# Attention and two feed-forward layers on one core: a planner that models the VectorE and GpSimd lock and traced durations, with 233 recorded priority moves in place of 400 random draws

## The chip, the core and the metric

One core of a Trainium2 chip runs the whole program in one launch. The metric is device time in microseconds (us). TensorE (PE) multiplies matrices, VectorE (DVE), ScalarE (ACT) and GpSimd (POOL) do elementwise work, and SyncE (SP) issues all transfers between main memory and on-chip memory. Each engine works through its own instructions in the order in which they were written; semaphores hold an instruction until what it needs is there.

## The reference

The inputs are q, k and v of shape (4, 8, 576, 64), and the weights of two layers for 2304 tokens of width 512:

```python
q_rot, k_rot = (rotate(q), rotate(k))
scores = scale * np.matmul(q_rot, k_rot.transpose(0, 1, 3, 2))
scores = scores - np.max(scores, axis=-1, keepdims=True)
attn = np.exp(scores)
attn = attn / (np.sum(attn, axis=-1, keepdims=True) + 1e-09)
x = np.matmul(attn, v)        # then heads side by side: (2304, 512)
h = (x @ w1) * (x @ w2) @ w3  # width 1024
x = h @ w_out                 # width 512
h = max(x @ u1, x @ u2, x @ u3)   # width 768
return h @ u_out
```

rotate turns the two halves of each head's 64 columns by position-dependent angles. The second layer's weights are called u here. The weights are 64-bit floats.

## The kernel before, in words

**Precision.** A value is kept as two parts, HI (the value cast to fp32r) and LO (the rest), and a product takes three matmuls (TERMS, HI x HI, LO x HI and HI x LO). So nearly every matrix is split once: a ScalarE cast for HI, and a subtraction on VectorE or GpSimd for LO. The 64-bit weights are turned into 32-bit floats by `convert` (lines 365 to 392) and `to_f32` (from line 749): a load of 512 KB, a ScalarE operation on the high words (line 383), a VectorE shift of the low words (line 385) and a VectorE shift and or (line 387; lines 759 and 761 in `to_f32`), and then the split (lines 389 and 391).

**Stages.** The attention works on 16 pairs of heads (4 batches of 4). For each, `prepare` rotates q and k (lines 490 and 492) and splits them (496, 497; line 500 copies a corner with GpSimd), `score` multiplies them into two score banks, VectorE takes the row maximum (538) and ScalarE the exponential (541), which leaves its row sum by a second instruction. `move` transposes the probabilities on TensorE (546) and splits them into `pt` by ScalarE (583) and VectorE (584), and `values` multiplies `pt` with v into `pv`; `collect`, `inverse` and `rows_done` scale and split the result. What TensorE does between these steps is other work that is ready: `fold` multiplies w_out by w3 beforehand (the folds), and `gates` computes (x @ w1) * (x @ w2) of a batch as soon as its four pairs are done, and stores it. After the attention come the remaining folds (line 711 on), `y_unit` (the folded matrix times the gates), `u_group` (the second layer by Strassen's scheme with 7 products, lines 906 to 933) and the output product, which ScalarE copies out at line 992. All matmuls carry line 320 of a helper, all transfers line 323.

**What sets the order.** The kernel writes no engine's order by hand. Every step is a task of a class `Plan`: an engine, a duration in us, what it reads and writes, and a priority. `Plan.order` (line 135) plays the tasks through a model: each engine takes the ready task of lowest priority number, a task ends after its duration, a transfer ends after a latency and a time by its size (lines 190 to 193), and the shared banks of the accumulation memory are given out as they come free. `Plan.issue` (line 219) plays the model 400 times with randomly changed priorities, keeps the order whose last TensorE task ends first in the model, and writes the instructions in that order. The same order sets which task gets which bank. All this happens while the program is built. The functions at lines 257 to 275 give durations by columns. Which engine does a task is fixed (`either`, line 362). Buffers are rings: a task that would overwrite a buffer waits for all the users of its last content, SyncE's loads included.

```python
dma = max(dma, end + 0.65) + 1.4 * k.tail
end = dma + 2.8
```

Of the kernel before, what the change touches and what calls it, by code (L numbers as in the profile page):

```python
# [45 lines left out]

class Task:
    __slots__ = ("eng", "dur", "emit", "prio", "tail", "deps", "after", "out", "next", "fresh", "shared", "num")
# [29 lines left out]
class Plan:  # L78
# [9 lines left out]
    ORDERS = 400  # L88
# [45 lines left out]

    def order(self, prio):
# [16 lines left out]
        dma, done = 0.0, []  # L152
# [3 lines left out]
        while len(done) < len(tasks):  # L156
# [17 lines left out]
            if k.fresh:  # L174
# [44 lines left out]
    def issue(self):  # L219
# [16 lines left out]
        draw = random.Random(0)  # L236
        best = prio = None
        for n in range(self.ORDERS):
            if n == 0:
                p = [k.prio for k in self.tasks]  # L240
            elif n < self.ORDERS // 5:
                by = draw.choice((0.05, 0.1, 0.2, 0.3))
                p = [k.prio + draw.gauss(0, by) for k in self.tasks]
            else:
                by, share = draw.choice((0.1, 0.3, 0.6)), draw.choice((0.003, 0.01, 0.03, 0.1))
                p = [x + draw.gauss(0, by) if draw.random() < share else x for x in prio]
            o = self.order(p)
            if o and (best is None or o[0] <= best[0]):
                best, prio = o, p
# [23 lines left out]
def c_pool(n):  # L273
    return 0.3 + 0.0022 * n
# [3 lines left out]
def fused_kernel(ctx, tc, qk, vv, cs, w3t, wo, w12, m2, wo2, out):  # L278
# [43 lines left out]
    def load(o, src, us, r=(), w=(), part=(), deps=(), prio=0.0):  # L322
        return add("SP", .5, lambda: sync.dma_start(o(), src()), r, w, part, deps, prio, tail=us)  # L323
# [41 lines left out]
    def convert(src, dst, c, prio, ring=None):  # L365
# [12 lines left out]
        def cols():  # L378
# [3 lines left out]
        early = ring is None and len(cw_r.all) <= 28  # L382
        add("ACT", 0.68, lambda: act.activation(w.t, hi_word().bitcast(F32), **SHRINK),
            r=[raw], w=[w], prio=prio)
        add("DVE", 0.85 if early else 0.43, lambda: dve.tensor_scalar(low_word(), low_word(), 29, None, ALU.logical_shift_right),  # L385
            part=[raw], deps=raw.writers, prio=prio)
        add("DVE", 1.15 if early else 0.69, lambda: dve.scalar_tensor_tensor(  # L387
            u(), u(), 3, low_word(), ALU.logical_shift_left, ALU.bitwise_or), r=[raw], w=[w], prio=prio)
# [3 lines left out]
            r=[w, dst], part=[dst], prio=prio)  # L392

    def split(dst, sel, n, prio, eng="DVE"):
# [5 lines left out]
            r=[dst], part=[dst], deps=dst.writers[-1:], prio=prio)  # L400
# [58 lines left out]
    for z in zs:  # L459
        add("POOL", 0.3, lambda z=z: pool.memset(f32(z.t), 0.0), w=[z], prio=-1)  # L460
# [4 lines left out]
    def prepare(p):  # L465
# [5 lines left out]
        for e in (1, 0):  # L471
# [12 lines left out]
            if p == 0 and e == 0:  # L484

                for i in range(2):
# [4 lines left out]
                        r=[tb[i]], part=[t], deps=[get[i]], prio=prio) for i in range(2)]  # L491
            k = add(eng, cost(S), lambda t=t, on=on: on.tensor_tensor(t.t[:, 0], t.t[:, 0], t.t[:, 1], ALU.add),
                    part=[t], deps=last, prio=prio)
# [4 lines left out]
                st.t[:, lo], t.t[:, 0], f32(st.t[:, hi]), ALU.subtract), part=[t, st], deps=[k], prio=prio)  # L498
# [4 lines left out]
    def prepare_v(p):  # L503
# [6 lines left out]
            r=[r, v], part=[v], prio=prio)  # L510
# [4 lines left out]
    def score(p, part, j):  # L515
# [16 lines left out]
        add("PE", 6 * c_mm(288) + (0.0 if common else 0.2), go, r=[st, z] if common else [st], w=ss, prio=prio)  # L532
        for e, s in enumerate(ss):
# [7 lines left out]
            add("ACT", 0.84, lambda s=s, col=col, o=o: act.activation(  # L541
# [208 lines left out]
    def to_f32(srcs, prio):  # L750
# [3 lines left out]
        for src, n in srcs:  # L754
# [4 lines left out]
        add("DVE", 0.5, lambda: dve.tensor_scalar(raw.t[:, :, 0], raw.t[:, :, 0], 29, None, ALU.logical_shift_right),  # L759
            part=[raw], deps=raw.writers, prio=prio)  # L760
        add("DVE", 0.87, lambda: dve.scalar_tensor_tensor(
            w.t.bitcast(U32), w.t.bitcast(U32), 3, raw.t[:, :, 0], ALU.logical_shift_left, ALU.bitwise_or),
            r=[raw], w=[w], prio=prio)
# [29 lines left out]
    def u_weights(n, w, t):  # L793
        prio = P2 + (7 if n < 2 else 20) + n
        d = us[n] = next_slot([128, 2, 7, 128], "u")
        for sel, lo, hi, src in ((lambda: w.t[:, :384], 0, 3, w), (lambda: t.t, 3, 7, t)):
# [4 lines left out]
                r=[src], part=[d], deps=[k], prio=prio)  # L801
# [5 lines left out]
    def y_unit(at, u):  # L807
# [27 lines left out]
        for kk in range(2):  # L835
# [22 lines left out]
            for t, c, deps in ((x, S1, [ks1, ks3]), (z, S2, [ks2, ks4])):  # L858
# [4 lines left out]
                    part=[yc], deps=[k], prio=prio)  # L863
# [20 lines left out]
    def u_group(n, grp, at):  # L884
# [43 lines left out]
        def out(o, e, t):  # L928
# [4 lines left out]
            add("DVE", c_dve(TN), lambda: dve.tensor_tensor(t.t, t.t, e.t, ALU.max), r=[e], w=[t], prio=prio)  # L933
# [130 lines left out]
```

## Time and profile before

| | |
|---|---|
| median of 3 runs (lowest to highest) | 942.92 us (942.62 to 944.05) |
| the profiled execution | 944.48 us |
| its span, first to last instruction | 942.5 us |
| instructions | 16352 |
| TensorE matmul busy | 898.9 us (95%), 6018 |
| TensorE weight loads busy | 835.4 us (89%) |
| VectorE busy | 613.3 us (65%), 1048 |
| ScalarE busy | 493.5 us (52%), 1108 |
| GpSimd busy | 398.6 us (42%), 387 |
| mean granted TensorE clock | 0.992 |

The profiled execution is one of its own; its span is what the engines show, and 1.98 us lie around it. Busy time counts an instruction from its start to its end. Matmuls are pipelined, so the next one starts while the one before still counts as busy, and a busy TensorE is not one at its peak. The time of a VectorE or GpSimd instruction includes what it waits for inside the engine. Of a wait the profile tells which instruction, as far as semaphores show, ended it. Granted clock 1.00 is 2.4 GHz, 0.50 is 1.2 GHz.

### The profile page before, as it was taken

Reading aid. Unit: us, or ns where it says so; the run is one execution under the profiler, and the core shown is the slowest. Engines: PE = TensorE matmul, PEld = TensorE weight load, DVE = VectorE, ACT = ScalarE, POOL = GpSimd, SP = SyncE. Lnnn points to the kernel's source line nnn. Section 1 sums busy time; section 2 is a strip of 40 time slices with the busy share of each in tenths; the row PEclk is TensorE's granted clock in tenths of the full one; section 3 lists DMA queues with packets and bytes.
Section 4 is the critical chain, followed back from the end, with each engine's and each line's share of the span. In section 5 each row is a group of like instructions: output and inputs, shape, how many; then the busy total and the mean of one; then the engine's idle time right before and its main releaser. Section 6 shows DMA issues by size and latency. Waiting matters only on the chain.

```text
span 942.5 us, 16352 instructions
## 1 busy us (share of the span) xinstructions
PE 898.9 (95%) x6018; PEld 835.4 (89%) x6018; DVE 613.3 (65%) x1048; ACT 493.5 (52%) x1108; POOL 398.6 (42%) x387
## 2 busy tenths in 40 slices
PE   2789999999999999999999999999989999999998
PEld 1667778889999999899998999999989999999886
DVE  6888989887666665666657332656687577588300
ACT  4688887776666665766644232434432322334411
POOL 1788889756665455632110000424563333342000
PEclk9799999999999999999999999999999999999999
DMA  7444556453232122210128543333233214155511
GB/s 250 129 152 144 163 156 199 152 155 113 99 96 85 59 85 89 97 40 27 34 101 254 181 133 101 92 102 96 67 112 112 79 46 137 54 174 185 201 68 67
DMA packets 61088, 110.32 MB, mean 117 GB/s; under 512 B 6736, under 2 KB 39760, under 8 KB 61008
## 3 DMA queue, kind: packets, MB, share of 16 engines
q1 hardware_dynamic: 61008, 109.28, 36.5%
q8 instruction: 47, 0.77, 0.3%
q14 instruction: 33, 0.27, 0.1%
HBM read 83.76 MB, written 25.50 MB: 116 GB/s over the span
## 4 chain that ended last, share of the span: by engine, by line
PE 79%; DVE 11%; ACT 5%; issue 3%; DMA 1%; POOL 1%; SPq 0%; DVEq 0%; ACTq 0%
PE q L320 45%; PE m L320 15%; PE t L546 7%; PE s L320 6%; PE pv L320 6%; DVE pt L584 3%; DVE sm L538 2%; ACT pt L583 2%; DVE cw L387 1%; DVE raw L385 1%; DMA tabs__119<-in_cs_dram 1%; POOL ga L784 1%; SPq L323 0%; DVE sm L551 0%; DMA r_d<-rt 0%
## 5 line engine op out<-in xcount | busy, mean ns | idle before, releaser
L584 DVE TENSOR_TENSOR pt<-t,pt 128x320 fp32r<-128x320 f32 (+3 forms) x256 | 132.6, 527 | 66.5 <-ACT pt L583 62.7
L583 ACT CAST pt<-t 128x320 fp32r<-128x320 f32 (+3 forms) x256 | 112.8, 457 | 54.1 <-PE t L546 35.2
L538 DVE TENSOR_REDUCE sm<-s 128x1 f32<-128x576 f32 x144 | 104.0, 750 | 17.1 <-PE s L320 16.0
L320 PE MATMUL pv<-pt,v 128*128 128x256 f32 (+1 forms) x576 | 110.3, 313 | 4.5 <-DVE pt L584 4.5
L320 PE MATMUL q<-gt,wp 128*128 128x384 f32 x576 | 100.0, 334 | 0.0
L320 PEld LDWEIGHTS q<-gt,wp 128*128 128x128 f32 x576 | 99.8, 188 | 0.0
L320 PE MATMUL s<-st 64*128 64x288 f32 x768 | 73.2, 319 | 19.0 <-ACT st L496 13.2
L320 PEld LDWEIGHTS pv<-pt,v 128*128 128x128 f32 x576 | 83.1, 191 | 8.9 <-DVE pt L584 6.1
L320 PEld LDWEIGHTS s<-st 64*128 64x128 f32 x768 | 56.4, 193 | 32.3 <-ACT st L496 13.2
L906 ACT COPY tmp<-q 128x384 f32<-128x384 f32 x54 | 25.9, 479 | 100.7 <-PE q L320 100.1
L320 PE MATMUL q<-yc__7826,u 128*128 128x384 f32 x378 | 70.8, 339 | 1.0 <-DVE tmp L932 1.0
L320 PE MATMUL q<-yc__8092,u 128*128 128x384 f32 x378 | 70.6, 339 | 1.1 <-DVE top L909 1.1
L320 PE MATMUL q<-yc__7547,u 128*128 128x384 f32 x378 | 71.1, 339 | 0.5 <-DVE tmp L909 0.4
L320 PEld LDWEIGHTS q<-yc__8092,u 128*128 128x128 f32 x378 | 66.6, 188 | 1.8 <-DVE top L909 1.5
L320 PEld LDWEIGHTS q<-yc__7826,u 128*128 128x128 f32 x378 | 66.7, 188 | 1.3 <-DVE tmp L932 1.3
L320 PEld LDWEIGHTS q<-yc__7547,u 128*128 128x128 f32 x378 | 66.2, 188 | 1.8 <-DVE tmp L909 0.7
L919 POOL TENSOR_TENSOR tmp<-tmp 128x384 f32<-128x384 f32 x27 | 29.8, 1103 | 89.9 <-ACT tmp L906 89.9
L320 PE MATMUL q<-tail,tail 128*128 128x512 f32 x216 | 49.1, 389 | 0.0
L320 PEld LDWEIGHTS q<-tail,tail 128*128 128x128 f32 x216 | 40.6, 188 | 8.4
L398 DVE TENSOR_TENSOR gt<-gt 128x768 fp32r<-128x768 f32 x24 | 25.5, 1068 | 27.0 <-ACT gt L397 27.0
L847 POOL TENSOR_TENSOR yx<-yc__7547 128x384 f32<-128x384 f32 x2 | 2.7, 1338 | 89.5 <-DVE yc__7547 L831 87.3
L992 ACT COPY ga<-q 128x512 f32<-128x512 f32 x18 | 10.6, 588 | 56.6 <-PE q L320 48.5
(1282 smaller groups left out, 2173.7 us busy)
## 6 DMA issues: line engine op xcount, KB each, us to landing
gt<-g_d SPq DMA_DIRECT2D x24, 384.0 KB
raw<-in_m_dram SPq DMA_DIRECT2D x72, 128.0 KB
raw<-in_w_dram SPq DMA_DIRECT2D x16, 512.0 KB
h_d<-top SPq DMA_DIRECT2D x36, 192.0 KB
tail<-h_d SPq DMA_DIRECT2D x36, 192.0 KB
raw<-in_wo_dram SPq DMA_DIRECT2D x12, 512.0 KB
raw<-in_w3t_dram SPq DMA_DIRECT2D x12, 512.0 KB
vr<-in_vv_dram SPq DMA_DIRECT2D x16, 320.0 KB
```

The lines of the kernel that those rows point to most:

```text
L320: pe.matmul(o, a, b, start=start, stop=stop, **kw)
L385: add("DVE", 0.85 if early else 0.43, lambda: dve.tensor_scalar(low_word(), low_word(), 29, None, ALU.logical_shift_right), part=[raw], de ...
L387: add("DVE", 1.15 if early else 0.69, lambda: dve.scalar_tensor_tensor(u(), u(), 3, low_word(), ALU.logical_shift_left, ALU.bitwise_or), r ...
L398: add(eng, c_dve(n) if eng == "DVE" else c_pool(n), lambda: e.tensor_tensor(sel()[:, LO], f32(sel()[:, LO]), f32(sel()[:, HI]), ALU.subtract),
L538: add("DVE", c_dve(S), lambda s=s, col=col: dve.tensor_reduce(sm.t[:, 0, col:col + 1], s.t[:, :, :288], axis=AX.XY, op=ALU.max, negate=Tru ...
L546: pe.transpose(o, x, ident.t)
L583: h = add("ACT", c_evac(n), lambda: act.copy(hi(), t.t[:rows, a:a + n]), r=[t], w=[pt], prio=prio)
L584: add("DVE", c_dve(n), lambda: dve.tensor_tensor(low(), t.t[:rows, a:a + n], f32(hi()), ALU.subtract), r=[t], part=[pt], deps=[h], prio=prio)
L784: return add("POOL", c_pool(128), lambda: pool.tensor_tensor(q(i), x(), y(), ALU.subtract), r=[w], part=[t], deps=deps, prio=prio)
L906: add("ACT", c_evac(TN), lambda: act.copy(d.t, ps(o)), r=[accs[o]], w=[d], prio=prio)
L919: add("POOL", c_pool(TN), lambda: pool.tensor_tensor(s5.t, s1.t, s5.t, ALU.add), r=[s1], w=[s5], prio=prio)
L992: add("ACT", c_evac(512), lambda acc=acc, o=o: act.copy(o.t, acc.t), r=[acc], w=[o], prio=P2 - 2)
```

## The change

Three things change, all in the planner. (1) A task may be marked `lock`: all GpSimd tasks but the two first fills are, and of VectorE's tasks those that work from on-chip main memory to it (the splits from it, the conversions, the rotation, the maxima of line 933, the small addition of line 551). In the model a marked task starts only when the marked task before it has ended, on whichever engine. (2) Durations: GpSimd by columns, the conversions, the exponential, a pair of scores, the small addition, an issue by SyncE, and the model of a transfer. (3) In place of 400 random draws the priorities are changed by 233 recorded moves, each given by a seed: a seed picks a stretch of the order, a share of its tasks and how far their priorities go. Then one order is played and written. The same tasks stay on the same engines. The diff, cut (some 20 more lines only add `lock=True`):

```diff
--- before.py
+++ after.py
@@ -1,5 +1,4 @@
-import random
@@ -44,8 +43,67 @@
+MOVES = (
+    100000004, 100000005, 100000020, 100000029, 100000035, 100000038, 100000041, 100000063, 100000085, 100000086,
...
+    100172746, 100174918, 100175949,
+)
+
+
+def draws(seed):
+    mask = (1 << 64) - 1
+    s = (seed * 0xD1342543DE82EF95 + 1) & mask
+    while True:
+        s = (s + 0x9E3779B97F4A7C15) & mask
+        z = ((s ^ (s >> 30)) * 0xBF58476D1CE4E5B9) & mask
+        z = ((z ^ (z >> 27)) * 0x94D049BB133111EB) & mask
+        yield z ^ (z >> 31)
+
+
+def move(prio, place, seed):
+
+    d = draws(seed)
+
+    def uni():
+        return (next(d) >> 11) * (1.0 / 9007199254740992.0)
+
+    by = (0.1, 0.3, 0.6, 1.5)[next(d) >> 62]
+    share = (0.01, 0.03, 0.1, 0.3)[next(d) >> 62]
+    parts = (1, 8, 32, 128)[next(d) >> 62]
+    width = len(prio) / parts
+    lo = uni() * (len(prio) + width) - width
+    hi = lo + width
+    if parts == 1:
+        share *= 0.3
+    for i in range(len(prio)):
+        if lo <= place[i] < hi and uni() < share:
+            x = uni() + uni() + uni() + uni() - 2.0
+            prio[i] = prio[i] + by * 1.7 * x
+
+
...
-    ORDERS = 400
...
-    def add(self, eng, dur, emit, r=(), w=(), part=(), deps=(), prio=0.0, tail=0.0):
+    def add(self, eng, dur, emit, r=(), w=(), part=(), deps=(), prio=0.0, tail=0.0, lock=None):
...
+        k.lock = eng == "POOL" if lock is None else lock
...
-        dma, done = 0.0, []
+        dma, port, done = 0.0, 0.0, []
...
+            if k.lock:
+                at = max(at, port)
             end = at + k.dur
+            if k.lock:
+                port = end
             clock[e] = end - LAP[e]
             if e == "PE":
                 end += self.DRAIN
             if k.tail:
-                dma = max(dma, end + 0.65) + 1.4 * k.tail
-                end = dma + 2.8
+                dma = max(dma, end + 0.65) + 1.2 * k.tail
+                end = dma + 0.8
...
-        draw = random.Random(0)
-        best = prio = None
-        for n in range(self.ORDERS):
...
+        prio = [k.prio for k in self.tasks]
+        place = {k.num: i for i, k in enumerate(self.order(prio)[1])}
+        for seed in MOVES:
+            move(prio, place, seed)
+        best = self.order(prio)
...
 def c_pool(n):
-    return 0.3 + 0.0022 * n
+    return 0.18 + 0.00216 * n
...
-        return add("SP", .5, lambda: sync.dma_start(o(), src()), r, w, part, deps, prio, tail=us)
+        return add("SP", .42, lambda: sync.dma_start(o(), src()), r, w, part, deps, prio, tail=us)
...
-        early = ring is None and len(cw_r.all) <= 28
...
-        add("DVE", 0.85 if early else 0.43, lambda: dve.tensor_scalar(low_word(), low_word(), 29, None, ALU.logical_shift_right),
-            part=[raw], deps=raw.writers, prio=prio)
-        add("DVE", 1.15 if early else 0.69, lambda: dve.scalar_tensor_tensor(
-            u(), u(), 3, low_word(), ALU.logical_shift_left, ALU.bitwise_or), r=[raw], w=[w], prio=prio)
+        add("DVE", 0.42, lambda: dve.tensor_scalar(low_word(), low_word(), 29, None, ALU.logical_shift_right),
+            part=[raw], deps=raw.writers, prio=prio, lock=True)
+        add("DVE", 0.69, lambda: dve.scalar_tensor_tensor(
+            u(), u(), 3, low_word(), ALU.logical_shift_left, ALU.bitwise_or), r=[raw], w=[w], prio=prio, lock=True)
...
-        add("PE", 6 * c_mm(288) + (0.0 if common else 0.2), go, r=[st, z] if common else [st], w=ss, prio=prio)
+        add("PE", 6 * c_mm(288) + (0.0 if common else 0.285), go, r=[st, z] if common else [st], w=ss, prio=prio)
...
-            add("ACT", 0.84, lambda s=s, col=col, o=o: act.activation(
+            add("ACT", 0.93, lambda s=s, col=col, o=o: act.activation(
...
-        a = add("DVE", 0.4, lambda: dve.tensor_scalar_add(sm.t[:, 2], sm.t[:, 1], EPS), r=[sm], part=[sm], prio=prio)
+        a = add("DVE", 0.17, lambda: dve.tensor_scalar_add(sm.t[:, 2], sm.t[:, 1], EPS), r=[sm], part=[sm], prio=prio,
+                lock=True)
...
-        add("DVE", 0.5, lambda: dve.tensor_scalar(raw.t[:, :, 0], raw.t[:, :, 0], 29, None, ALU.logical_shift_right),
-            part=[raw], deps=raw.writers, prio=prio)
-        add("DVE", 0.87, lambda: dve.scalar_tensor_tensor(
...
+        add("DVE", 0.42, lambda: dve.tensor_scalar(raw.t[:, :, 0], raw.t[:, :, 0], 29, None, ALU.logical_shift_right),
+            part=[raw], deps=raw.writers, prio=prio, lock=True)
+        add("DVE", 0.69, lambda: dve.scalar_tensor_tensor(
```

## Rows read from the trace of the kernel before

**Rows 1.** Busy time by stage: stretch and length, engines, granted clock, transfer share, GB/s.

```profile
0.00:75.00 75.00, 47.65 (x303) 38.98 (x304) 59.15 (x93) 49.98 (x113) 46.27 (x45) 0.91 0.52 170
75.00:200.00 125.00, 119.10 (x892) 102.86 (x890) 109.19 (x182) 101.22 (x244) 105.11 (x87) 1.00 0.55 169
200.00:490.00 290.00, 285.93 (x2325) 266.85 (x2325) 189.49 (x365) 190.21 (x482) 136.19 (x128) 1.00 0.23 75
490.00:660.00 170.00, 169.99 (x1036) 165.68 (x1035) 87.69 (x128) 61.59 (x105) 27.61 (x26) 1.00 0.47 142
660.00:705.00 45.00, 42.40 (x235) 40.56 (x235) 35.84 (x59) 18.69 (x37) 28.38 (x36) 1.00 0.31 94
705.00:943.00 238.00, 233.81 (x1235) 220.46 (x1233) 131.98 (x226) 71.81 (x131) 55.07 (x68) 1.00 0.33 111
```

The engines stand in the order PE, PEld (weight loads), DVE, ACT, POOL.

**Rows 2.** Waits of PE, 0 to 75 us: for whom, us in total, times, longest.

```profile
PE s L320 <- ACT st L496: 13.2, 1, 13.2
PE pv L320 <- DVE pt L584: 3.2, 5, 1.9
PE s L320 <- ACT p__209 L541: 2.5, 1, 2.5
PE s L320 <- ACT p__176 L541: 1.7, 1, 1.7
```

**Rows 3.** Waits of PE, 75 to 200 us.

```profile
PE t L546 <- DVE pt L584: 3.4, 7, 1.3
```

**Rows 4.** Waits of PE, 490 us to the end.

```profile
PE q L320 <- DVE top L909: 1.1, 1, 1.1
PE q L320 <- DVE tmp L932: 1.0, 1, 1.0
```

**Rows 5.** Instructions in order of time: start, duration, engine, idle before it.

```profile
27.84 0.28 POOL L500 CAST z__105<-st 64x128 fp32r<-64x128 f32 x1
27.87 2.20 DVE L387 SCALAR_TENSOR_TENSOR cw<-cw,raw 128x512 uint32<-128x512 uint32 x1
28.09 1.42 POOL L490 TENSOR_TENSOR qk__169<-qk__169,tabs__131 128x576 f32<-128x576 f32 x1
...
30.10 1.14 DVE L584 TENSOR_TENSOR pt<-t,pt 64x256 fp32r<-64x256 f32 x2
...
32.61 0.74 ACT L541 ACTIVATE p__314<-s,sm 128x576 f32<-128x576 f32 x1 [0.70 <-DVE sm L538]
...
33.24 0.19 ACT L541 ACTIVATION_READ_ACCUMULATOR p__314<-s,sm 128x1 f32 x1
...
34.10 1.22 PE L320 MATMUL pv<-pt,v 128*128 128x256 f32 x4 [1.95 <-DVE pt L584]
```

**Rows 6.** Conversions by line: busy us, mean ns; 0 to 75, 75 to 200, last 490 on.

```profile
L387 DVE SCALAR_TENSOR_TENSOR cw<-cw,raw 128x512 uint32<-128x512 uint32 x8 | 9.6, 1195 | 0.2
L385 DVE TENSOR_SCALAR raw<-raw 128x512 uint32<-128x512 uint32 x8 | 6.7, 843 | 0.1
...
L387 DVE SCALAR_TENSOR_TENSOR cw<-cw,raw 128x512 uint32<-128x512 uint32 x20 | 21.2, 1059 | 3.7 <-ACT cw L383 3.2
L385 DVE TENSOR_SCALAR raw<-raw 128x512 uint32<-128x512 uint32 x19 | 18.6, 984 | 0.1
...
L387 DVE SCALAR_TENSOR_TENSOR cw<-cw,rawc 128x512 uint32<-128x512 uint32 x6 | 4.1, 691 | 2.1 <-ACT cw L383 1.9
...
L385 DVE TENSOR_SCALAR rawc<-rawc 128x512 uint32<-128x512 uint32 x6 | 2.5, 421 | 0.0
```

**Rows 7.** Busy time by stretch, columns as in rows 1: the clock after a stall.

```profile
32.00:34.00 2.00, 0.16 (x2) 0.00 (x0) 1.96 (x5) 1.39 (x4) 2.00 (x3) 0.85 0.38 150
34.00:36.00 2.00, 1.90 (x10) 1.67 (x12) 1.86 (x4) 1.10 (x4) 0.86 (x1) 0.50 0.03 8
```

**Rows 8.** Instructions in order of time: a load's issue and its first use.

```profile
543.96 0.37 SPq L323 DMA_DIRECT2D gt<-g_d  x1
...
547.14 0.83 ACT L397 CAST gt<-gt 128x768 fp32r<-128x768 f32 x1 [2.29 <-DMA gt<-g_d]
```

More of the change, by code (lines that the diff above doesn't have):

```diff
@@ L43 @@
 TERMS = ((HI, HI), (LO, HI), (HI, LO))
+MOVES = (
[24 rows of a table added]
+)
[23 more added lines that the diff above has]
+            prio[i] = prio[i] + by * 1.7 * x
 class Task:
-    __slots__ = ("eng", "dur", "emit", "prio", "tail", "deps", "after", "out", "next", "fresh", "shared", "num")
+    __slots__ = ("eng", "dur", "emit", "prio", "tail", "deps", "after", "out", "next", "fresh", "shared", "num", "lock")
 class Buf:
@@ L235, in issue @@
                 d.next.append(k)
-        draw = random.Random(0)
-        best = prio = None
-        for n in range(self.ORDERS):
[L239 to L249, printed above, removed]
+        prio = [k.prio for k in self.tasks]
[3 more added lines that the diff above has]
+        best = self.order(prio)
         for b, n in best[2].items():
@@ L391, in convert @@
         add(eng, cost(512), lambda: on.tensor_tensor(cols()[:, LO], w.t, f32(cols()[:, HI]), ALU.subtract),
-            r=[w, dst], part=[dst], prio=prio)
+            r=[w, dst], part=[dst], prio=prio, lock=True)
     def split(dst, sel, n, prio, eng="DVE"):
@@ L399, in split @@
             sel()[:, LO], f32(sel()[:, LO]), f32(sel()[:, HI]), ALU.subtract),
-            r=[dst], part=[dst], deps=dst.writers[-1:], prio=prio)
+            r=[dst], part=[dst], deps=dst.writers[-1:], prio=prio, lock=True)
     wob = [slots[4 + i].new() for i in range(2)]
@@ L459, in fused_kernel @@
     for z in zs:
-        add("POOL", 0.3, lambda z=z: pool.memset(f32(z.t), 0.0), w=[z], prio=-1)
+        add("POOL", 0.3, lambda z=z: pool.memset(f32(z.t), 0.0), w=[z], prio=-1, lock=False)
     QH, QL, KH, KL = range(4)
@@ L490, in prepare @@
             last = [add(eng, cost(S), lambda i=i, t=t, on=on, tb=tb: on.tensor_tensor(t.t[:, i], t.t[:, i], tb[i].t, ALU.mult),
-                        r=[tb[i]], part=[t], deps=[get[i]], prio=prio) for i in range(2)]
+                        r=[tb[i]], part=[t], deps=[get[i]], prio=prio, lock=True) for i in range(2)]
             k = add(eng, cost(S), lambda t=t, on=on: on.tensor_tensor(t.t[:, 0], t.t[:, 0], t.t[:, 1], ALU.add),
-                    part=[t], deps=last, prio=prio)
+                    part=[t], deps=last, prio=prio, lock=True)
             eng, cost, on = either(p < 1)
@@ L497, in prepare @@
             add(eng, cost(S), lambda t=t, on=on, hi=hi, lo=lo: on.tensor_tensor(
-                st.t[:, lo], t.t[:, 0], f32(st.t[:, hi]), ALU.subtract), part=[t, st], deps=[k], prio=prio)
+                st.t[:, lo], t.t[:, 0], f32(st.t[:, hi]), ALU.subtract), part=[t, st], deps=[k], prio=prio, lock=True)
         for e, rows in enumerate(HEADS):
@@ L509, in prepare_v @@
         add(eng, cost(640), lambda: on.tensor_tensor(v.t[:, :, LO], r.t, f32(v.t[:, :, HI]), ALU.subtract),
-            r=[r, v], part=[v], prio=prio)
+            r=[r, v], part=[v], prio=prio, lock=True)
     probs = {}
@@ L758, in to_f32 @@
             r=[raw], w=[w], prio=prio)
[L759 to L761 removed]
+        add("DVE", 0.42, lambda: dve.tensor_scalar(raw.t[:, :, 0], raw.t[:, :, 0], 29, None, ALU.logical_shift_right),
+            part=[raw], deps=raw.writers, prio=prio, lock=True)
+        add("DVE", 0.69, lambda: dve.scalar_tensor_tensor(
             w.t.bitcast(U32), w.t.bitcast(U32), 3, raw.t[:, :, 0], ALU.logical_shift_left, ALU.bitwise_or),
[L763 removed]
+            r=[raw], w=[w], prio=prio, lock=True)
         return w
@@ L800, in u_weights @@
                 d.t[:, LO, lo:hi], sel().rearrange("p (a b) -> p a b", b=128), f32(d.t[:, HI, lo:hi]), ALU.subtract),
-                r=[src], part=[d], deps=[k], prio=prio)
+                r=[src], part=[d], deps=[k], prio=prio, lock=True)
     yc_r = [ring("py", [128, 7, 2, 2, TN], F32R, f"yc{g}_") for g in range(NG)]
@@ L862, in y_unit @@
                     yc.t[:, c:c + 2, kk, LO], t.t[:, 1:3], f32(yc.t[:, c:c + 2, kk, HI]), ALU.subtract),
-                    part=[yc], deps=[k], prio=prio)
+                    part=[yc], deps=[k], prio=prio, lock=True)
                 t.users += [k, k2]
@@ L932, in out @@
             add("DVE", c_dve(TN), lambda: dve.tensor_tensor(e.t, ps(o), e.t, ALU.add), r=[accs[o]], w=[e], prio=prio)
-            add("DVE", c_dve(TN), lambda: dve.tensor_tensor(t.t, t.t, e.t, ALU.max), r=[e], w=[t], prio=prio)
+            add("DVE", c_dve(TN), lambda: dve.tensor_tensor(t.t, t.t, e.t, ALU.max), r=[e], w=[t], prio=prio, lock=True)
         prod("c", S4, B22, 4)
```

22 rows, old and new, of the table MOVES are left out of this document.

## The prediction

> **What bounds the kernel now.** I read the stages first. From 490 us on TensorE is full: idle for 0.01 us of 170 up to 660, 2.6 us of 45 up to 705, and 3.7 us after that, which is the last copy and store [rows 1]. No order of the same 16,352 instructions shortens that half by more than some 2.6 us. What an order can win lies in the first 490 us, the attention: TensorE is idle for 27.35 us up to 75, 5.9 up to 200 and 4.1 up to 490. Of the first 27.35, 13.2 are the head, until the first operands are loaded, rotated and split [rows 2]; that chain uses the same loads and the same operations after the change.
>
> A busy TensorE is pipelined, so short waits hide in its busy time. I therefore compare paces. In 200 to 490 a matmul leaves every 290/2325 = 0.1247 us, its own waits included [rows 1]. At that pace the 303 matmuls up to 75 need 37.8 us; between 13.2 and 75 they took 61.8, so about **24.0 us** are lost there. The 892 up to 200 need 111.2 and took 125: **13.8 us**. (The kinds differ a little between the stretches; it is an estimate.)
>
> Then what ended those waits: the exponential that frees a score bank, and the low half of the transposed probabilities, `pt`, from VectorE line 584 [rows 2, 3]. Why line 584 is late shows in order of time [rows 5]: at 27.87 VectorE begins a weight conversion, line 387. GpSimd runs line 500 and then line 490, and the conversion ends only at 30.07. Two `pt` behind it start at 30.10 and TensorE still waits for VectorE at 34.1, 1.95 us visibly. Alone, that conversion takes 0.691 and its partner on line 385 0.421; beside GpSimd they average 1.195 and 0.843 up to 75, and 1.059 and 0.984 from 75 to 200 [rows 6]. The surplus is VectorE time spent waiting for GpSimd: 8 x 0.504 + 8 x 0.422 = 7.4 us up to 75, and 20 x 0.368 + 19 x 0.563 = 18.1 us up to 200. VectorE is busy 59 of 75 and 109 of 125 us there, so this is time on the engine that TensorE waits for. A stall costs twice: after TensorE stood nearly idle at 32 to 34 the granted clock is 0.50 at 34 to 36, the 1.2 GHz level [rows 7].
>
> **The change, part by part.** It adds and removes no instruction: every engine does the same work, each in another order. The planner runs while the kernel is built, so neither 400 drawn orders nor the replay of 233 moves costs chip time. All terms are waits that go or come.
>
> *The lock in the model.* A task that is marked starts only when the last marked one has ended, on either engine. Before, two conversions were given fixed inflated times (0.85 and 1.15 for the early ones), so the planner thought VectorE slow but could not see which GpSimd operation to avoid. Now it sees 0.42 and 0.69 plus a wait that depends on the order. The order can set the conversion before a `pt` that is not yet needed, or two locked VectorE operations side by side. The bounds of the gain in each stretch are nothing (GpSimd is busy 46 and 105 us there and the lock must be shared somehow) and the whole loss.
> - Up to 75: between 0 and 24.0. The nearest row is the surplus of the 8 conversions, 7.4 us. I take **7.0**.
> - 75 to 200: between 0 and 13.8. The surplus, 18.1, is above the loss, so the rows do not choose; GpSimd is busy 84% of the time and will keep colliding. I take half, **7.0**.
> - 200 to 490: idle is 4.1. Few conversions are left, but the same `pt` waits end it. I take **3.0**; bounds 0 and 4.1.
> - 660 to 705: 2.6 idle, with waits for line 909's and 932's results [rows 4]. I take **1.5**; bounds 0 and 2.6.
> - 490 to 660 and after 705: nothing; TensorE's queue covers all of it, and if a late load broke that cover the wait would show there one for one.
>
> *Durations.* The exponential goes from 0.84 to 0.93; its two records are 0.74 and 0.19 [rows 5]. GpSimd on 576 columns goes from 0.3 + 0.0022 x 576 = 1.57 to 1.42; the record is 1.42. These correct the order and carry no term of their own; their worth is inside the four terms, since the waits that remain come from the old figures too.
>
> *Transfers.* For a 384 KB load the model counted 0.5 + 0.65 + 1.4 x 1.1 + 2.8 = 5.49 us from issue to use; now 0.42 + 0.65 + 1.2 x 1.1 + 0.8 = 3.19. The trace has issue at 543.96 and use at 547.14: 3.18 us [rows 8]. So loads that come through a clear queue are modelled right now and may be used 2.3 us earlier. SyncE issues in order: behind a load that waits for its buffer stand all later ones, the stores of the gates too. Up to 200 the transfer engines are busy about 54% of the time [rows 1], so some loads will land later than the model says. Bounds: 0 if all were early anyway, and 2.3 us for each load that becomes the last thing ScalarE waits for. I take 0: TensorE's waits name no transfer anywhere beyond the head [rows 2 to 4].
>
> **Sum.** 7.0 + 7.0 + 3.0 + 1.5 = 18.5 us. The profiled execution took 944.48 (span 942.5, with 1.98 around it); it would take 926.0, span 924.0. The median of the runs is 942.92, 1.56 below the profiled one, so I forecast 942.92 - 18.5 = **924.4**.
>
> **Rivals.**
> *More is won.* Waits hidden by the pipeline go too, and the low clock after 34 with them: 16 of 24.0 (the first scores and `pt` of pair 0, some 8 us, have nothing to hide behind), 12 of 13.8, 4 of 4.1, 2.5 of 2.6, together 34.5: 908.4. For it: weight loads are idle for 290 - 266.85 = 23.2 us in 200 to 490, where TensorE seems idle for only 4.1 [rows 1]. Against: a long matmul keeps the next weight load waiting with nothing wrong. The Trainium skill (Trainium Kernel Development and Optimization, Performance Expectations) says that matmul busy time is a bad measure because matmuls are pipelined, and weight-load busy time a good one; by that rule alone more lies open in 200 to 490 than my 4.1, and this case would be the likelier.
>
> *Less is won.* The opening is bound by throughput: VectorE 59 of 75, GpSimd 105 and VectorE 109 of 125 [rows 1], and the folds and gates that could fill TensorE need those conversions. Then 2 + 3 + 1 + 1 = 7: 935.9. Against: ScalarE and GpSimd do stand idle in both stretches.
>
> *No change.* Waits go to other places one for one, because TensorE waits for the last of four engines. 942.9. It would also be so if the replayed moves gave an order no better than the old.
>
> *Slower: the lock passes VectorE by.* The model gives the lock in the order of asking, so a marked VectorE task waits for at most the GpSimd task then running. The row shows otherwise: asked at 27.87, GpSimd's line 500 ended at 28.12, but line 490 got in at 28.09 and VectorE ended at 30.07, against 28.12 + 0.69 = 28.81: 1.26 us later [rows 5]. An order that packs GpSimd without gaps and sets conversions just ahead of `pt` makes this happen more often, in the first 200 us. Each case holds VectorE 1.26 us with `pt` queued behind and TensorE behind that; 18.5/1.26 = 15 additional cases cancel the gain, 25 give 31.5 - 18.5 = 13 us more: 955.9. Against: line 387's mean of 1.195 up to 75 says that most cases wait for one task at most. The Trainium skill (SBUF — State Buffer, Who interferes with whom) states that whoever issues first gets the shared ports for the whole instruction; by that rule VectorE would have had them at 28.12 and this rival could not occur, but the row at 27.87 does not fit it.
>
> **How the numbers follow.** The forecast 0.55 (913 to 932: half as much again or half of the terms), more 0.15, less 0.17, no change 0.04, slower 0.09. Faster by over 0.2%, about what a measurement of this kernel can tell from no change: 0.87; within: 0.04; slower: 0.09. The range, 908 to 938, holds the first three cases with a little above the third, and leaves out the last two, 0.13.
>
> **What would show it.** In the profile after: the same busy ScalarE; VectorE's busy time shorter, with lines 385 and 387 nearer 0.42 and 0.69 up to 200; TensorE's idle up to 200 down from 33 us to 20 or so; few stretches at 0.50 after 30 us; 490 to 660 still full, ending earlier by the same amount. If lines 385 and 387 take as long as before and the time still falls, the lock was not the reason and the search or the durations were. If ScalarE's first waits are for loads up to 200, the transfer figures are too short. If conversions over 1.7 us are frequent, the lock rival is right. I am wrong in size if the stretch before 75 does not shrink.

## The result, and the profile after

The changed kernel took 933.17 us (932.24 to 935.18, 4 runs), the kernel before 943.48 on the same chip: a ratio of 0.9893, 95% interval 0.9872 to 0.9914. That is **10.3 us faster**; the forecast was 18.5 faster, at 924.4. Direction and range (908 to 938) held, the size was little over half: the time lies 1.2 us outside the band that had the most weight (913 to 932) and nearer to the rival "less is won" (935.9) than to the forecast.

Busy time by stage of the kernel after, columns and stretches as in [rows 1]; its span is 931.7 us:

```profile
0.00:75.00 75.00, 44.97 (x275) 35.65 (x275) 58.19 (x85) 46.89 (x105) 46.56 (x45) 0.91 0.50 169
75.00:200.00 125.00, 121.52 (x930) 107.70 (x930) 107.09 (x192) 105.32 (x255) 102.17 (x84) 1.00 0.54 174
200.00:490.00 290.00, 288.56 (x2373) 273.03 (x2372) 192.69 (x373) 194.87 (x490) 141.49 (x131) 1.00 0.26 82
490.00:660.00 170.00, 169.56 (x1021) 165.50 (x1020) 86.40 (x127) 62.60 (x105) 34.43 (x32) 1.00 0.41 126
660.00:705.00 45.00, 45.00 (x257) 45.00 (x256) 35.62 (x65) 17.97 (x35) 21.68 (x32) 1.00 0.33 99
```
(The stage from 705 us on is left out: TensorE is idle there for the last 3.6 us, as before.)

Read it by TensorE's idle time and by its matmuls beside [rows 1]. Idle, in the order of the stages: 30.0 (27.35 before), 3.5 (5.9), 1.4 (4.1), 0.4 (0.01), 0 (2.6). Matmuls done: at 75 us 275, 28 **fewer** than before; at 200 us 1205, 10 more; at 490 us 3578, 58 more; at 705 us 4856, 65 more. So the opening lost time, and the rest won back more than three times as many matmuls.

The kinds of matmul that are done early differ, so counts are only a guide to times. An estimate that weighs them: count each matmul with the planner's own duration for its columns (`c_mm`: 0.013 us and 0.000417 us for each column, at least 0.109). By that measure the changed kernel's TensorE is 3.6 us of work **behind** the kernel before at 75 us, and ahead by 1.5 at 200, 7.8 at 490, 7.4 at 660, 11.1 at 705 and 10.7 at its last matmul. Stage by stage that is -3.6, 5.1, 6.3, -0.4, 3.7 and -0.4 us. In the second profile of the same order (the run `again` below) it is -2.0 at 75 us and 9.5 at the end, so a single profile is good to a microsecond or two.

TensorE's waits, after, 0 to 75 us and below the dots 75 to 200 us; beside [rows 2, 3]:

```profile
PE s L373 <- ACT st L548: 13.1, 1, 13.1
PE s L373 <- ACT p__349 L593: 4.2, 2, 3.0
PE s L373 <- ACT p__208 L593: 3.4, 1, 3.4
PE t L598 <- DVE sm L605: 2.9, 2, 2.2
...
PE pv L373 <- DVE pt L637: 1.7, 2, 1.4
PE t L598 <- DVE pt L637: 0.6, 1, 0.6
```

From 75 to 200 us, the `t` waits for `pt` fall from 3.4 us in seven waits to 0.6 in one; the `pv` waits for `pt` do not fall (1.3 us before, 1.7 after). Up to 75 the waits for two score banks (`p__349`, `p__208`) alone cost 7.6 us, as much as all the waits for score banks before (7.3, the longest 2.5).

The conversions, after, 0 to 75 us and then 75 to 200 us, beside [rows 6]; lines 437 and 439 are the old 385 and 387:

```profile
L439 DVE SCALAR_TENSOR_TENSOR cw<-cw,raw 128x512 uint32<-128x512 uint32 x7 | 7.7, 1097 | 0.1
L437 DVE TENSOR_SCALAR raw<-raw 128x512 uint32<-128x512 uint32 x8 | 6.5, 829 | 0.1
...
L439 DVE SCALAR_TENSOR_TENSOR cw<-cw,raw 128x512 uint32<-128x512 uint32 x20 | 19.2, 962 | 0.9 <-ACT cw L435 0.7
L437 DVE TENSOR_SCALAR raw<-raw 128x512 uint32<-128x512 uint32 x20 | 13.8, 692 | 1.6 <-DMA raw<-in_w_dram 1.3
```

Against 0.691 and 0.421 alone, the surplus up to 75 us is 7 x 0.406 + 8 x 0.408 = 6.1 us (7.4 before), and from 75 to 200 us 20 x 0.271 + 20 x 0.271 = 10.8 (18.1 before; 12.4 in the second profile). The collisions cost less but are far from gone.

The longest of the new waits, in order of time:

```profile
16.87 0.81 DVE L542 TENSOR_TENSOR early<-early,tabs__107 128x576 f32<-128x576 f32 x1
17.48 1.47 POOL L542 TENSOR_TENSOR qk__146<-qk__146,tabs__107 128x576 f32<-128x576 f32 x1 [0.41 <-DMA qk__146<-in_qk_dram]
17.61 1.97 DVE L542 TENSOR_TENSOR early<-early,tabs__115 128x576 f32<-128x576 f32 x1
18.92 1.91 POOL L542 TENSOR_TENSOR qk__146<-qk__146,tabs__115 128x576 f32<-128x576 f32 x1
19.49 1.95 DVE L542 TENSOR_TENSOR early<-early,tabs__134 128x576 f32<-128x576 f32 x1
21.36 1.41 DVE L590 TENSOR_REDUCE sm<-s 128x1 f32<-128x576 f32 x2
22.14 0.74 ACT L593 ACTIVATE p__208<-s,sm 128x576 f32<-128x576 f32 x1 [3.70 <-DVE sm L590]
...
24.70 0.41 PE L598 MATMUL t<-ident,p__182 128*128 128x128 f32 x1
...
26.12 0.27 PE L598 MATMUL t<-ident,p__208 128*128 128x128 f32 x1
```

VectorE does three products in a row. A load lands just before 17.48, GpSimd starts on it while the first product runs, takes the lock, and from then on the two engines take turns: the second and third product take 1.97 and 1.95 us instead of 0.75. (The plan has this GpSimd product at 18.83, behind VectorE's three.) The row maxima behind them come 2.4 us late, then the exponential that frees the bank, then TensorE.

### The profile page after: what moved, and what is told of

Its sections match the earlier page's. It is cut to its first block, busy times and chain, and to the rows that moved or that the text cites. A ratio compares the mean times of both kernels' runs of the same rounds, so it can differ in the third digit from the quotient of the medians.

```text
span 931.7 us, 16391 instructions
## 1 busy us (share of the span) xinstructions
PE 892.7 (96%) x6018; PEld 836.9 (90%) x6018; DVE 601.5 (65%) x1048; ACT 495.5 (53%) x1108; POOL 397.6 (43%) x387
## 4 chain that ended last, share of the span: by engine, by line
PE 86%; DVE 6%; ACT 2%; DMA 2%; issue 2%; POOL 1%; SPq 0%; DVEq 0%; ACTq 0%
PE q L373 46%; PE m L373 17%; PE t L598 9%; PE s L373 7%; PE pv L373 7%; DVE sm L590 1%; DVE pt L637 1%; ACT pt L636 1%; DVE cw L439 1%; DMA qk__118<-in_qk_dram 1%; DMA raw<-in_w_dram 1%; DVE raw L437 1%; DMA wq_d<-fl 1%; DVE early L542 0%; DMA wp<-wq_d 0%
## 5 line engine op out<-in xcount | busy, mean ns | idle before, releaser
L373 PE MATMUL pv<-pt,v 128*128 128x256 f32 (+1 forms) x576 | 115.4, 317 | 4.5 <-DVE pt L637 3.6
L590 DVE TENSOR_REDUCE sm<-s 128x1 f32<-128x576 f32 x144 | 104.2, 749 | 17.3 <-PE s L373 16.4
L985 DVE TENSOR_TENSOR tmp<-q,tmp 128x384 f32<-128x384 f32 x54 | 29.8, 554 | 16.3 <-PE q L373 16.2
L1045 ACT COPY ga<-q 128x512 f32<-128x512 f32 x18 | 10.6, 588 | 54.8 <-PE q L373 46.7
```

Of the source, the lines that this page charges most:

```text
L373: pe.matmul(o, a, b, start=start, stop=stop, **kw)
L590: add("DVE", c_dve(S), lambda s=s, col=col: dve.tensor_reduce(sm.t[:, 0, col:col + 1], s.t[:, :, :288], axis=AX.XY, op=ALU.max, negate=Tru ...
L985: add("DVE", c_dve(TN), lambda: dve.tensor_tensor(e.t, ps(o), e.t, ALU.add), r=[accs[o]], w=[e], prio=prio)
L1045: add("ACT", c_evac(512), lambda acc=acc, o=o: act.copy(o.t, acc.t), r=[acc], w=[o], prio=P2 - 2)
```

## Experiments

### Is it the opening? A lock lost to an early load, and a low clock

Three kernels add work to the changed one and leave its order alone. The first holds GpSimd back, so that VectorE's three products run together; the second fills TensorE's wait at 35 to 38 us with transposes whose results nothing reads, to keep the clock from falling; the third does both.

```diff
+    def hold():
+        t = ap.tile([128, 512], F32, tag="hold", name="hold")
+        for _ in range(4):
+            pool.memset(t, 0.0)
...
+    def warm():
+        t = ps_m.tile([128, 512], F32, tag="bank1", name="warm")
+        for i in range(24):
+            tr(t[:, 128 * (i % 4):128 * (i % 4) + 128], ident.t)
...
         for k in best[1]:
+            if k.eng == "POOL":
+                count += 1
+                if count == 6:
+                    self.hold()
+            if k.eng == "PE":
+                turns += 1
+                if turns == 18:
+                    self.warm()
             k.emit()
```

> The changed kernel itself, so that the three kernels beside it have a baseline on the same chip. Every theory expects 0.989 of the kernel before, about 933 us, with the same profile: conversions short from 75 us on, and up to 75 us TensorE no faster than before.

> Added work only: four fills of an unused tile on GpSimd, some 2.1 us, ahead of its first rotation product at 17.48 us. Theory: a load that landed 1.35 us before the model's time let GpSimd start early and take the lock inside VectorE's planned run of three products, which took 0.81, 1.97 and 1.95 us. With GpSimd held back they take 0.75 each, TensorE's wait at 23.1 us falls from 3.4 us to about 1, and the end comes 2 to 2.6 us earlier than in the changed kernel (ratio to it 0.997 to 0.998). Rival: GpSimd is what the opening waits for; then 2.1 us more on it cost 1 to 2 us, or the gain is given back within 50 us and the ratio is 1.000.

> Added work only: 24 transposes of the identity matrix into an unused bank, in TensorE's wait between 35.4 and 38.4 us. Theory: the stall at 36 to 38 us costs a second time, because the granted clock is 0.50 from 38 to 50 us and some 9 us of matmuls take double there. With TensorE kept busy the clock stays at 1.00 and the end comes 3 to 4 us earlier (ratio to the changed kernel 0.996 to 0.997). Rival: VectorE and ScalarE set the pace up to 75 us; then the clock rises, but TensorE waits instead, and the gain is under 1 us.

> The two additions together: GpSimd held back ahead of its first rotation product and TensorE kept busy at 35 to 38 us. If both theories hold and do not share their gain, 5 to 6.5 us less than the changed kernel (ratio 0.993 to 0.995); if the opening is bound by VectorE and ScalarE, under 1.5 us.

Ratios to the kernel before, with intervals: the changed kernel again 0.9901 (0.9886 to 0.9915), 933.51 us; held 0.9893 (0.9878 to 0.9908), 933.47; warm 0.9888 (0.9871 to 0.9904), 932.97; both 0.9881 (0.9863 to 0.9898), 931.31. The intervals overlap, so none of the additions has a measured gain. With both, the median is 2.2 us below the changed kernel's, between what the theory (5 to 6.5) and the rival (under 1.5) expected, and not clear of noise. But both additions did what they were to do. The held kernel in order of time:

```profile
16.94 2.27 POOL L389 MEMSET hold<- 128x512 f32 x4
17.53 0.74 DVE L554 TENSOR_TENSOR early<-early,tabs__115 128x576 f32<-128x576 f32 x1
18.20 0.74 DVE L554 TENSOR_TENSOR early<-early,tabs__134 128x576 f32<-128x576 f32 x1
19.46 1.42 DVE L602 TENSOR_REDUCE sm<-s 128x1 f32<-128x576 f32 x2 [0.52 <-PE s L378]
21.23 1.78 PE L378 MATMUL s<-st,z__105 128*128 128x288 f32 x6 [1.57 <-ACT p__213 L605]
```

The products take 0.74, and TensorE starts the batch at 21.23 instead of 23.15. What became of it shows where TensorE starts the same matmul (counted from the first, added transposes left out) in the profile of each, in us:

| matmul | again | hold | warm | both |
|---|---|---|---|---|
| 25 | 23.15 | 21.23 | 21.36 | 21.49 |
| 139 | 49.98 | 48.75 | 47.68 | 46.32 |
| 240 | 65.76 | 65.26 | 63.55 | 63.78 |
| 294 | 75.83 | 74.97 | 75.16 | 74.98 |
| 1205 | 200.19 | 198.25 | 200.50 | 198.26 |
| 5947 | 912.82 | 911.34 | 912.18 | 912.23 |

At 50 us the two additions have won 3.7 us; at 76 us 0.7 to 0.9 is left, whichever was made. These are single profiles: the first profile of the changed kernel starts its 294th matmul at 76.67, 0.84 later than the one in the table, so differences of a microsecond or two, further down above all, rank nothing. Busy time by stretch of the kernel with both:

```profile
36.00:38.00 2.00, 1.00 (x7) 0.55 (x5) 2.00 (x4) 2.00 (x5) 0.62 (x1) 1.00 0.30 40
40.00:45.00 5.00, 3.11 (x26) 2.50 (x27) 4.03 (x7) 3.43 (x9) 5.00 (x5) 1.00 0.75 236
...
68.00:70.00 2.00, 0.97 (x5) 1.00 (x6) 2.00 (x4) 0.83 (x2) 1.55 (x3) 0.70 0.84 223
70.00:72.00 2.00, 2.00 (x7) 1.51 (x6) 1.27 (x2) 1.81 (x5) 2.00 (x2) 0.50 0.58 231
```

and two of its instructions in order of time:

```profile
69.03 0.37 PE L615 MATMUL t<-ident,sm 128*9 128x128 f32 x1 [2.16 <-DVE sm L629]
...
69.69 2.79 PE L383 MATMUL m<-ws__177,ws__588 128*128 128x512 f32 x6
```

The same stretches in the changed kernel run again (but the first):

```profile
40.00:45.00 5.00, 3.85 (x19) 3.01 (x19) 3.16 (x6) 3.23 (x9) 5.00 (x4) 0.50 0.79 265
...
68.00:70.00 2.00, 0.96 (x4) 0.48 (x3) 1.94 (x3) 0.63 (x2) 2.00 (x2) 1.00 0.81 235
70.00:72.00 2.00, 0.65 (x5) 0.66 (x6) 1.97 (x5) 0.83 (x2) 1.62 (x4) 1.00 0.88 256
```

and the same wait and six matmuls in it:

```profile
71.35 0.27 PE L598 MATMUL t<-ident,sm 128*9 128x128 f32 x1 [2.38 <-DVE sm L605]
...
71.70 1.64 PE L373 MATMUL m<-ws__177,ws__558 128*128 128x512 f32 x6
```

The clock stays at 1.00 through 36 to 45 us, where it had been 0.50. TensorE then comes earlier to its wait for VectorE's `sm`, which is its 258th matmul, and that wait too ends earlier, at 69.03 instead of 71.35. So of the 3.7 us 2.3 are left there: VectorE is ahead as well. Behind the wait the granted clock falls to 0.50, and six matmuls take 2.79 instead of 1.64; that takes 1.5 of the 2.3. A low clock was removed at one place and another came. Why it came there is open: the changed kernel stands idle at the same wait for as long (2.38 us, against 2.16) with the clock shown as 1.00 throughout, and so does the held kernel (2.14), while behind the same wait of the kernel with the transposes only (2.40) it is shown as 0.62 and 0.53.

The rival held in its result: most of the time that was won by 50 us is given back within 30 us. Of its reason, that up to 75 us TensorE follows VectorE, ScalarE and GpSimd, the profiles show a part, the 1.3 us that go between 50 us and the wait; the other 1.5 went with the clock.

One more thing shows in the run with the transposes only: VectorE got its second product through without any help (0.75 us; the third still took 1.96), and matmul 25 starts at 21.36. Everything before had come half a microsecond earlier. So not all that this run wins up to 50 us is due to its transposes, which start only at 34.42.

### Model or search?

Four kernels with the planner's search made equal: 20,000 tries of the same kind of move, each kept where it makes the planned end earlier. They differ in the model alone.

```diff
 # eq_both_new: MOVES are the 53 kept of 20,000
 # eq_no_lock: the lock is off while the moves are tried and in the order that is written
-            if k.lock:
+            if k.lock and self.LOCK:
                 at = max(at, port)
 # eq_old_durations: the lock stays
-    return 0.18 + 0.00216 * n
+    return 0.3 + 0.0022 * n
-        return add("SP", .42,
+        return add("SP", .5,
-                dma = max(dma, end + 0.65) + 1.2 * k.tail
-                end = dma + 0.8
+                dma = max(dma, end + 0.65) + 1.4 * k.tail
+                end = dma + 2.8
...
 # eq_old_model: both, and the inflated conversions of before
```

> The changed planner with a search of its own: 20,000 tried moves of the same kind, 53 of them kept, in place of the recorded 233. The control for the three beside it, which have the same number of tries. Every theory expects nearly what the changed kernel gives, 0.990 to 0.993 of the kernel before (934 to 937 us).

> The traced durations without the lock in the model, 20,000 tries, 48 kept. If the lock is what counts: VectorE's conversions take 0.9 to 1.2 us again up to 200 us and the time is 0.997 or more of the kernel before (940 us or more). If the traced durations or the search count, 0.990 to 0.993 like the control.

> The lock in the model, but the durations and the transfer figures of before (without the inflated conversions, which stood for the lock), 20,000 tries, 61 kept. If the traced durations count: 0.997 or more of the kernel before. If the lock or the search counts: 0.990 to 0.993.

> The planner's model of before, without the lock and with the old durations, but 20,000 tries in place of 400, 53 kept. If the number of tries is what counts: 0.990 to 0.993 of the kernel before. If the model counts: 0.998 to 1.002, because 50 times the search then only follows a wrong model.

Two more with the changed model and less search: no moves at all, and the 400 draws of before.

> The changed model with no move replayed: one order from the priorities as written. If the model alone made the gain, 0.990 to 0.995 of the kernel before; if the moves are needed to use it, 1.005 to 1.02, because the kernel before had the best of 400 orders and this has the first.

> The changed model, but the 400 random draws of the kernel before in place of the 233 moves. If the model is what counts and a short search is enough: 0.990 to 0.994 of the kernel before. If the recorded moves are worth as much as the model: 0.995 to 1.000.

| kernel | model | search | us | ratio (95%) | TensorE's end: planned, profiled |
|---|---|---|---|---|---|
| before | old | 400 draws | 943.48 | 1 | 914.3, 938.8 |
| after | new | 233 moves | 933.17 | 0.9893 (0.9872 to 0.9914) | 912.6, 928.1 |
| eq_old_model | old | 20,000 | 941.79 | 0.9979 (0.9969 to 0.9988) | 907.4, 936.4 |
| no_moves | new | none | 957.19 | 1.0142 (1.0125 to 1.0159) | 935.0, 952.5 |
| draws_400 | new | 400 draws | 950.45 | 1.0080 (1.0058 to 1.0103) | 928.4, 948.4 |
| eq_both_new | new | 20,000 | 933.69 | 0.9894 (0.9878 to 0.9911) | 915.8, 928.0 |
| eq_old_durations | lock, old durations | 20,000 | 947.79 | 1.0041 (1.0028 to 1.0055) | 933.4, 943.1 |
| eq_no_lock | new durations, no lock | 20,000 | 957.52 | 1.0136 (1.0113 to 1.0159) | 906.0, 951.7 |

(The last column has the end of the last TensorE task in the plan that the kernel computes while it is built, and the end of the last matmul in its profile, in us.)

Four things follow. Search alone brought 0.2%: under the old model 20,000 tries in place of 400 give 0.9979. The model alone brought nothing: with the 400 draws of before it is 0.8% **slower** than before, which neither expectation had. Together they give the whole gain, and 53 moves from 20,000 tries give as much as the 233 recorded ones. And neither half of the model did: with the durations traced but the lock left out the kernel is 1.4% slower than before. A likely reason is that the durations of before had inflated the conversions to stand for the lock, and that stand-in is gone; no run puts it back alone.

One reservation goes with all four. Each kernel is one order, found by one search, and its interval tells how well that order was timed, not how much the next search would differ. Under "Can more be had?" orders of the same or nearly the same model lie 5.2 and 9.6 us apart from the ones here. So the 24 us of eq_no_lock stand well clear of that, the 14 of eq_old_durations less so, and the 8 of eq_old_model do not.

TensorE's waits from 75 to 200 us in eq_no_lock:

```profile
PE t L581 <- DVE pt L620: 8.3, 9, 1.9
PE t L581 <- DVE sm L588: 3.8, 2, 2.5
```

the busy time of that stage in it:

```profile
75.00:200.00 125.00, 108.55 (x771) 92.84 (x769) 104.85 (x171) 93.99 (x223) 94.85 (x76) 0.96 0.53 165
```

and the first two stages of eq_both_new:

```profile
0.00:75.00 75.00, 50.66 (x321) 40.91 (x322) 61.36 (x94) 51.97 (x117) 51.88 (x48) 0.93 0.56 187
75.00:200.00 125.00, 119.11 (x903) 104.86 (x901) 105.60 (x184) 100.99 (x245) 101.04 (x84) 1.00 0.53 164
```

Without the lock the stage up to 200 us gets 771 matmuls done where the changed kernel gets 930. And eq_both_new has 321 done at 75 us, 46 more than the changed kernel, and ends at the same time: the count at 75 us says little of the end.

Nor do short conversions make the gain. The rows from 75 to 200 us in eq_both_new and, below the dots, in eq_old_model:

```profile
L421 DVE SCALAR_TENSOR_TENSOR cw<-cw,raw 128x512 uint32<-128x512 uint32 x20 | 20.3, 1018 | 0.8 <-ACT cw L417 0.7
L419 DVE TENSOR_SCALAR raw<-raw 128x512 uint32<-128x512 uint32 x19 | 15.5, 818 | 2.5 <-DMA raw<-in_w_dram 1.7 <-DMA raw<-in_w3t_dram 0.8
...
L422 DVE SCALAR_TENSOR_TENSOR cw<-cw,raw 128x512 uint32<-128x512 uint32 x19 | 18.9, 993 | 1.3 <-ACT cw L418 0.7
L420 DVE TENSOR_SCALAR raw<-raw 128x512 uint32<-128x512 uint32 x18 | 15.0, 834 | 0.2
```

The surplus is 14.1 us in the first, which has the whole gain, and 13.2 in the second, which has almost none. So what parts the two is not how long VectorE waits for GpSimd. It fits that only the first one's plan knows of those waits: TensorE ends 12.3 us behind its plan there and 29.0 in the other, though their durations differ as well.

How true each model is shows beside the plan that the kernel computes while it is built. The start of a matmul in the profile less the start of its task in the plan, in us, at about the same places:

| kernel | 50 us | 200 us | 485 us |
|---|---|---|---|
| before | 2.6 | 11.8 | 22.5 |
| after | 4.6 | 5.8 | 10.7 |

From 50 to 200 us, where conversions and GpSimd collide most, the kernel before falls 9.2 us behind its plan and the changed one 1.2. Up to 50 us the new plan is little truer: the first matmul comes 3.2 us before its place in the old plan and 0.6 behind it in the new, so by 50 us the one has fallen behind by 5.8 and the other by 4.0.

The two ends in the table above say it in one number. The changed kernel's plan ends only 1.8 us earlier than the plan before; its TensorE ends 10.7 us earlier. Nearly all of the gain is a plan that comes true, not a better plan. eq_no_lock shows the reverse: it has the shortest plan of all and ends 45.7 us behind it. But a true plan is not enough: eq_old_durations ends only 9.7 us behind its plan, the least of all, and the plan itself ends at 933.4.

### Can more be had?

A finer model (other transfer figures; TensorE at half its pace in the opening), and a longer search in the changed one.

```diff
 # finer_model, 62 kept of 20,000 tries
-                dma = max(dma, end + 0.65) + 1.2 * k.tail
-                end = dma + 0.8
+                dma = max(dma, end + 0.65) + 1.05 * k.tail
+                end = dma + 1.0
...
-            end = at + k.dur
+            end = at + k.dur * (2 if e == "PE" and at < 25.5 else 1)
 # longer_search: the 233 moves, then those of 37,500 more tries that did not make the planned end later
```

> The changed planner with two more measured things in its model: loads take less per byte and land a little later after that (1.05 and 1.0 in place of 1.2 and 0.8), and TensorE's durations are doubled up to 25.5 us, as its transposes show (0.42 us up to 26 us, 0.27 after). 20,000 tries, 62 moves kept. If what is left is error of the model in the first 50 us: 0.985 to 0.988 of the kernel before (929 to 932 us). If the opening is bound by VectorE, ScalarE and GpSimd together: 0.988 to 0.991, as the changed kernel.

> The changed kernel's moves and 37,500 more tries of the same kind after them, in the same model; moves that left its end equal were kept too, so that the order drifts. If the model is exact enough for more search to pay: 0.986 to 0.988 of the kernel before. If the search has run out, as 20,000 and 233 recorded moves giving the same time suggest: 0.988 to 0.991.

Neither theory expected this: the finer model gives 0.9993 (0.9983 to 1.0003), 943.31 us, and the longer search 0.9950 (0.9937 to 0.9962), 938.74. The longer search's runs spread from 935.36 to 940.02 (its profile is of the fastest), the changed kernel's from 932.24 to 935.18. Why is open. What the plans show: the longer search made the planned end 1.8 us earlier, 910.7, and TensorE ended 1.7 us **later**, 929.8; the finer model's plan ends at 914.0 and TensorE at 937.1. A search that goes on with an inexact model can shorten the plan and lengthen the kernel. The finer kernel changed two things at once and has a search of its own. By the measure of the last table its plan is 5.9 us behind at 116 us and 17.3 at 481, so it drifts long after 25.5 us, where only the transfers are modelled differently; that points to the transfer figures, but no run tells the parts apart, and the longer search, whose model is the changed kernel's, drifts too (4.9 at 165, 13.8 at 470). No version was found that is measurably faster than the changed kernel; the interval of the one with both additions, 931.31, overlaps its own.

## Why the prediction was right, and where it was off

The range held in part by luck. In the weighted measure of the first section the terms 7.0, 7.0, 3.0 and 1.5 came out as -3.6, 5.1, 6.3 and 3.7, with -0.4 in each of the two stretches that had none: the opening missed by 10.6, and two later stages gave 5.5 more than forecast.

**Bound.** Right in that the gain came before 705 us; TensorE's idle is 0.4 us of 170 up to 660 and 3.6 at the end. By the weighted measure the second half gave 2.9 us (2.2 in the second profile), about the 2.6 that the bound allowed.

**Up to 75 us: 7.0 forecast; this is the term that was mis-sized.** TensorE's idle there grew by 2.7 us, to 30.0, and 28 fewer matmuls are done (16 fewer in the second profile). The prediction had named this as its sign of being wrong in size. The step that failed is "At that pace the 303 matmuls up to 75 need 37.8 us ... about 24.0 us are lost there": it took a pace from a stage with other work to fill in as something that the opening could reach. No order here comes near it: that pace would give 495 matmuls by 75 us, and the most that any has is eq_both_new's 321. 3.7 us given to TensorE by 50 us were 0.85 at 76, and 46 more matmuls by 75 us in eq_both_new moved the end by nothing. This is what the rival "less is won" said of the opening, with a chance of 0.17, and at 7.0 forecast and some 28 x 0.1247 = 3.5 lost, 10.5 short (9.0 by the second profile), it is more than the 8.2 us by which the sum fell short. The signs that hung on it failed too: TensorE's idle up to 200 us did not fall (33.25 before, 33.5 after), and the clock is at 0.50 from 38 to 45 us.

**75 to 200 us: 7.0 forecast.** In the changed kernel it looks as told: surplus from 18.1 to 10.8 us, all waits for `pt` from 4.9 to 2.3. In counts TensorE goes from 28 behind to 10 ahead, 38 x 0.1247 = 4.7 us; weighted, 5.1. But that the shorter conversions are the cause is not shown: eq_both_new wins as much with a surplus of 14.1. The lock seems to count by what the plan knows of it more than by how seldom it is met.

**200 to 490 us: 3.0 forecast, bound 4.1.** 48 more matmuls, 6.0 us at that pace, of which 2.7 are idle time. Of the 4.1 us of idle, 1.7 were waits for `pt`; the prediction had put all of it down to them. The bound was too tight, since it counted visible idle alone; here the rule of the Trainium skill that the forecast set aside (Trainium Kernel Development and Optimization, Performance Expectations) read the stage better: idle of the weight loads fell from 23.2 to 17.0 us, by 6.2. The trace agrees in the other stages too: from stage to stage up to 705 us that idle fell by -3.3, 4.8, 6.2, -0.2 and 4.4 us, and the weighted work won was -3.6, 5.1, 6.3, -0.4 and 3.7.

**660 to 705 us: 1.5 forecast.** Idle from 2.6 to 0, and 3.7 us of work won: from 490 to 705 TensorE does 7 matmuls more, and longer ones.

**Durations without a term of their own.** No run tells their share from the lock's, but they matter: without them the lock, with a search of its own, gives 1.0041.

**Transfers at 0.** In the changed kernel TensorE still waits for none beyond the head. But a transfer decided the wait of 3.4 us at 23.1, and not by being late: it landed 1.35 us before its place in the plan and let GpSimd in. The forecast had not thought of that sign.

**The rival that the lock passes VectorE by.** It fell. In the changed kernel no VectorE instruction up to 200 us is longer than its time alone and one GpSimd task (the largest excess is 1.28 us, and GpSimd's 576-column products take 1.40); the row at 27.87 [rows 5] had no second of its kind before. The turn-taking at 17.61 and 19.49 is one wait each, and agrees with the rule of the Trainium skill (SBUF — State Buffer, Who interferes with whom) that whoever issues first has the ports.

**"No change" and "more".** Neither came. What the forecast never asked is which part of the change carries the gain; the runs answer, with one search for each, that each part alone brings 0.2% or a loss.

## What to carry to other kernels

When a static order is planned by a model, improve the model and then search anew, and compare the planned end with the measured one: here the gain was almost all in how far the plan came true. Right prices beside a missing cause gave a slower kernel here than wrong prices that stood in for it, and a better model searched as little as the old one was slower too. Price an opening by the engine that feeds it, not by the bottleneck engine's pace elsewhere: fill a wait for a trial and see where the time goes. And where two engines share a lock, a fixed order on each does not fix the order between them: here a load that came early delayed TensorE's batch at 23.15 by 1.9 us, and holding GpSimd back undid it.

## What was not expected of the hardware

- Two runs of one order took the lock differently: with GpSimd beginning at 17.42 and VectorE at 17.63, VectorE's product took 1.97 us; in the run with the transposes GpSimd began at 17.04 and VectorE at 17.05, and VectorE's took 0.75 while GpSimd's took 2.02. A few tenths of a microsecond decide over 1.2. (0.01 is finer than such records can rank, GpSimd's above all.)
- GpSimd's fills did not hold VectorE up: beside 2.27 us of them, from 16.94 on, the products took 0.74 us, where beside GpSimd's products they took 1.97 and 1.95.
- Work added to an engine (2.27 us of fills on GpSimd, 24 transposes on TensorE) did not lengthen the kernel: 0.9881 with both against 0.9901 without.
- The granted clock is shown as 1.00 up to 25 us, yet transposes take 0.41 us at 24.70 and 0.27 at 26.12, and 0.42 is also what they take in the kernel with both additions from 69.19 on, where the clock is shown as 0.50. In the opening the durations point to the 1.2 GHz level until then, which the clock column does not show.
